# Seven products of halves for the last three experts' first layer, and the first batch's keys and values summed on TensorE

## The chip, the cores and the metric

The program runs on one core of one Trainium2 chip. The metric is the device time of one execution in microseconds. TensorE (PE) multiplies matrices and writes its results to PSUM, which has eight banks here (the tiles `pa`). VectorE (DVE), ScalarE (ACT) and GpSimd (POOL) do the elementwise work; GpSimd's work is all on SBUF. SyncE (SP) issues most DMA transfers, GpSimd the gathers and scatters.

## What is computed

Three stages follow each other on 4608 tokens of width 512.

```python
k_p, v_p = k.reshape(B, H, Sp, 8, D).mean(axis=3), v.reshape(B, H, Sp, 8, D).mean(axis=3)   # B, H, S, D = 8, 8, 576, 64
attn = softmax(q @ k_p.T / sqrt(D)) @ v_p
h = x @ w_in                                     # 512 to 2048
g = (a0 + a1*h + a2*h**2 + a3*h**3) / (1 + |b0|*|h| + |b1|*h**2 + 1e-6)
x = g @ w_out                                    # 2048 to 512
# each token goes to one of 8 experts, by the sorted gate scores, 576 tokens to an expert
for e in range(8):
    out[mask] = relu(x[mask] @ w1[e]) @ w2[e]    # 512 to 1024 to 512
```

## The kernel before

The kernel writes every operation, with its engine, an estimated duration and what it reads and writes, into a list. A planner (`Order.run`) then plays the list through with those estimates and fixes the order on each engine: among the operations that are ready it takes the one with the lowest priority number, which is the place in the list unless `prio` says otherwise. An operation written with `either` (as in `tt` and `cp`) goes to whichever of two engines the planner finds better. PSUM banks are given out by the planner too (`Dyn`). Any change in the list can therefore move the order of the work everywhere. Where the plan shows TensorE idle early on, matmuls on a tile of zeros (line 348) are put in.

A product in full precision is made of three matmuls in the faster 32-bit format (fp32r): each operand is split into a rounded part h and a remainder l, and h*h, h*l and l*h are added up in PSUM. A rounding is a ScalarE copy, a remainder a subtraction on VectorE or GpSimd.

**The start.** The attention of a batch is done in two units of four heads. For a unit the kernel loads keys (`load_k`, 0.59 MB), values (`load_v`, 0.79 MB in two transfers for the first batch) and queries (`load_q`, 0.26 MB for 256 tokens). `prep_k` sums the keys over groups of 8 with one reduction on VectorE (line 535) and scales them into `kbd`; `prep_v` sums the first batch's values by halves in three steps on GpSimd (line 553) and one reduction on VectorE (line 555), then rounds them. Scores (line 589), the maximum (line 593), exponentials on ScalarE (line 602) and transposes (line 624) follow. Keys of all units share the buffer `kvraw`, so unit 1's keys are requested when unit 0's are summed. The queue begins with a piece of the weights (0.52 MB), keys, queries and values of unit 0; the constants `cst` (0.09 MB, with the identity matrix and the polynomial's coefficients) come later, by `LATER = 60`. Small operations on the coefficients (lines 387 to 394) need them. Beside the attention, the weights of the next stage are rebuilt piece by piece from 64-bit numbers (`prep_w`).

**The middle.** The polynomial stage runs as 2 x 72 steps, with `act1` and `act2` on each. `mt` is a ring of three tiles (`MTB`) and `mr` one of two, later three (`MRB`, `MORE_R`), for the low part of its quotient; `ex` is a ring of two (`EXB`) for the exponentials.

**The experts.** `ffn(k)` does expert k: a first layer, with hidden features on the partitions in eight blocks f of 128 and the 576 tokens in two halves of 256 and 320 columns, then a second layer over five tiles of tokens (four of 128, one of 64). For one f and half there are twelve matmuls:

```python
products = (wh, yh), (wh, yl), (wl, yh)
...
    nc.tensor.matmul(ps()[:, 0:n], w()[:, c, fs], x()[:, c, :], start=i == 0, stop=i == 11)
```

`load` fetches a quarter of a weight matrix (0.52 MB), rounds it on ScalarE (line 1833) and takes the remainder on GpSimd (line 1837). The first layer's output is rounded with the ReLU (line 1922), its remainder taken on VectorE (line 1927). `begin(k + 1)` loads the next expert's first-layer weights while expert k is worked on, `fetch(k + 1)` gathers its tokens and `turn` transposes them on TensorE and splits them (8 column groups a pair of tiles of 128 on VectorE). Both weight matrices have rings of five quarters, the split tokens two sets. `route(k + 1)`, the choice of the next expert's tokens, is a long chain on VectorE that runs ahead of the experts and ends before the last three. `out` is written by a scatter from `ob` (line 1975).

Of the kernel before, what the change touches and what calls it, by code (L numbers as in the profile page):

```python
# [18 lines left out]
ALU = mybir.AluOpType  # L19
# [21 lines left out]
LATER = 60  # L41
W_FIRST = 1
MTB = 3
# [9 lines left out]
EXB, ENB = (2, 4)  # L53
# [251 lines left out]
class Kern:  # L305
# [172 lines left out]
    def init_att(self):  # L478
# [4 lines left out]
        self.dma(lambda: self.cst()[:, 0:170], lambda: self.a["cst"], 87040, w=[self.vmask, self.ident, self.wgate, (self.scal, 0), (self.scal, 1)], prio=LATER)  # L483
# [49 lines left out]
    def prep_k(self, b, u):  # L533
        nc, op, k, ks = self.nc, self.op, self.kvraw, self.ks
        op("DVE", c_tt(1152), lambda: nc.vector.tensor_reduce(
            ks(), k()[:, 0:2 * S].rearrange("p (c s j) -> p c s j", c=2, j=8), op=ALU.add, axis=AX.X), r=[k] + [(k, r) for r in range(4)], w=[ks])
        h = self.kbd[u]
        for r in range(2):
            o = lambda r=r: h()[64 * r:64 * r + 64, :, NK * r:NK * r + NK]
            i = lambda r=r: ks()[64 * r:64 * r + 64]  # L540
# [3 lines left out]
    def prep_v(self, b, u):  # L544
        nc, op, v, vs, vf = self.nc, self.op, self.kvraw, self.vs, self.vf
        vk = [v] + [(v, r) for r in range(4)]
        if b == 0:
            v, x = self.vhead[u]
            n, f4 = 8, lambda: v().rearrange("p (c x) -> p c x", c=2)
            while n > 1:  # L550
                n //= 2
                o = (lambda n=n: f4()[:, :, 0:n * D]) if n > 1 else (lambda: vs()[:, 0:2])
                op("Pool", p_tt(2 * n * D), lambda o=o, n=n: nc.gpsimd.tensor_tensor(
                    o(), f4()[:, :, 0:n * D], f4()[:, :, n * D:2 * n * D], op=ALU.add), r=[v], w=[v] if n > 1 else [vs])
# [14 lines left out]
        for r in range(2):  # L569
            def z(t, r=r):  # L570
                return t()[64 * r:64 * r + 64, 0:2, 64 * r:64 * r + 64]
            sv = lambda r=r: vs()[64 * r:64 * r + 64, 0:2, :]
            op("Act", c_act(128, 1), lambda z=z, sv=sv: nc.scalar.activation(z(h), sv(), AF.Copy), r=[vs], w=[(h, r)])
# [85 lines left out]
    def att_slots(self):  # L659
# [7 lines left out]
        def first():  # L667
            self.load_k(0, 0)
            self.load_q(0)
            self.load_v(0, 0)  # L670
            self.prep_k(0, 0)
            self.load_k(0, 1)
            for i in range(1, QB):
                self.load_q(i)
            self.load_v(0, 1)
# [1163 lines left out]

    def begin(self, k):  # L1840
# [6 lines left out]
        self.w1 = []  # L1847
        for j in range(4):
# [6 lines left out]
    def fetch(self, k):  # L1855

        nc, fop, ix = self.nc, self.fop, self.ix[k % 3]
        for c in range(5):
# [31 lines left out]
    def ffn(self, k):  # L1890
# [3 lines left out]
        for j in range(4):  # L1894
            d = (self.w2h[self.n2 % 5], self.w2l[self.n2 % 5])
            self.n2 += 1
            w2.append(d)
# [185 lines left out]
```

## Time and profile before

| | us |
|---|---|
| median of 3 runs | 1479.06 (1478.07 to 1480.18) |
| the profiled execution | 1474.23 |
| its span in the profile | 1472.5 |
| TensorE busy | 1436.0 (98%) |
| VectorE busy | 1056.0 (72%) |
| ScalarE busy | 910.8 (62%) |
| GpSimd busy | 859.3 (58%) |

Times in the profile count from the start of the span. A busy TensorE is not TensorE at its peak: a matmul's row is longer than the distance to the next one, since they overlap, and what a matmul costs is read from the distance of the starts. VectorE's rows overlap a little too. The granted clock is 1.00 when TensorE runs at full speed. An idle engine that nothing waits for costs nothing.

### The profile page before, as it was taken

Reading aid. Unit: us, or ns where it says so; the run is one execution under the profiler, and the core shown is the slowest. Engines: PE = TensorE matmul, PEld = TensorE weight load, DVE = VectorE, ACT = ScalarE, POOL = GpSimd, SP = SyncE. Lnnn points to the kernel's source line nnn. Section 1 sums busy time; section 2 is a strip of 40 time slices with the busy share of each in tenths; the row PEclk is TensorE's granted clock in tenths of the full one; section 3 lists DMA queues with packets and bytes.
Section 4 is the critical chain, followed back from the end, with each engine's and each line's share of the span. In section 5 each row is a group of like instructions: output and inputs, shape, how many; then the busy total and the mean of one; then the engine's idle time right before and its main releaser. Section 6 shows DMA issues by size and latency. Waiting matters only on the chain. (4 is left out here: it accounts for less than half of the span.)

```text
span 1472.5 us, 27165 instructions
## 1 busy us (share of the span) xinstructions
PE 1436.0 (98%) x9476; PEld 1298.5 (88%) x9476; DVE 1056.0 (72%) x2894; ACT 910.8 (62%) x2206; POOL 859.3 (58%) x806
## 2 busy tenths in 40 slices
PE   8899989999999999999999999999999999999998
PEld 7899879888898999988999899777888988988997
DVE  6987787868778698887767777987877877731220
ACT  6998877878868787766545565843454553543331
POOL 6878777667757465664445654743374653753521
PEclk9999999999999999999999999999999999999999
DMA  7663533242421444433233332014154433533300
GB/s 252 217 226 110 177 125 123 88 145 92 151 91 51 144 132 146 137 87 97 77 116 99 103 86 88 1 59 162 61 163 147 155 130 98 165 116 114 129 26 32
DMA packets 105941, 173.61 MB, mean 118 GB/s; under 512 B 8384, under 2 KB 72256, under 8 KB 105792
## 3 DMA queue, kind: packets, MB, share of 16 engines
q1 hardware_dynamic: 80896, 134.02, 27.5%
q0 software_dynamic: 24896, 37.76, 9.1%
q8 instruction: 75, 1.23, 0.3%
q14 instruction: 74, 0.61, 0.1%
HBM read 122.29 MB, written 49.46 MB: 117 GB/s over the span
## 5 line engine op out<-in xcount | busy, mean ns | idle before, releaser
L735 PE MATMUL pa<-xh,wih 128*128 128x256 f32 (+1 forms) x576 | 202.9, 352 | 7.8 <-DVE mt L792 5.8
L735 PE MATMUL pa<-xh,wil 128*128 128x256 f32 (+1 forms) x576 | 195.3, 339 | 0.7 <-POOL wil L362 0.7
L735 PE MATMUL pa<-xl,wih 128*128 128x256 f32 (+1 forms) x576 | 194.7, 338 | 0.0
L860 PE MATMUL pa<-woh,mg 128*128 128x260 f32 x480 | 130.3, 287 | 1.1 <-DVE mg L782 1.0
L362 POOL TENSOR_TENSOR mg<-mt,mr 128x512 fp32r<-128x512 f32 x75 | 96.9, 1293 | 56.6 <-DVE mt L792 39.0
L861 PE MATMUL pa<-wol,mg 128*128 128x260 f32 x480 | 128.3, 283 | 0.0
L735 PEld LDWEIGHTS pa<-xh,wih 128*128 128x128 f32 x576 | 109.4, 190 | 20.3 <-DVE mt L792 5.1
L1975 POOL DMA_INDIRECT out<-ob,ix x40 | 38.9, 973 | 151.0 <-ACT ob L1971 127.2
L735 PEld LDWEIGHTS pa<-xh,wil 128*128 128x128 f32 x576 | 109.2, 190 | 13.6 <-POOL wil L362 0.9
L735 PEld LDWEIGHTS pa<-xl,wih 128*128 128x128 f32 x576 | 109.5, 190 | 8.6
L792 DVE SCALAR_TENSOR_TENSOR mt<-pa,cst,mt 128x512 f32<-128x512 f32 x144 | 107.0, 744 | 10.5 <-POOL mt L788 9.8
L753 ACT ACTIVATE ms<-pa,cst 128x512 f32<-128x512 f32 x72 | 49.3, 684 | 98.1 <-PE pa L735 98.1
L602 ACT ACTIVATE ex<-pa,nm 128x72 f32<-128x72 f32 (+2 forms) x320 | 99.1, 331 | 9.7 <-DVE nm L593 9.3
L858 PE MATMUL pa<-woh,mg 128*128 128x260 f32 x480 | 105.0, 285 | 0.0
L765 DVE TENSOR_TENSOR mwq<-mwq,pa 128x512 f32<-128x512 f32 x96 | 65.3, 683 | 44.7 <-ACT pa L759 22.8
L1922 ACT ACTIVATE h2h<-pa 128x256 fp32r<-128x256 f32 (+1 forms) x128 | 51.2, 407 | 71.0 <-PE pa L1919 66.5
L1927 DVE SCALAR_TENSOR_TENSOR h2l<-pa,h2h 128x256 fp32r<-128x256 f32 x128 | 53.3, 418 | 55.8 <-ACT h2h L1922 49.0
L860 PEld LDWEIGHTS pa<-woh,mg 128*128 128x128 f32 x480 | 90.4, 188 | 2.4 <-DVE mg L782 1.9
L362 POOL TENSOR_TENSOR en<-ex,sm 128x256 f32<-128x256 f32 (+5 forms) x160 | 77.9, 508 | 24.8 <-DVE sm L608 12.3
L861 PEld LDWEIGHTS pa<-wol,mg 128*128 128x128 f32 x480 | 90.5, 188 | 0.3
L781 ACT ACTIVATE mr<-mr,cst 128x512 f32<-128x512 f32 x121 | 88.3, 730 | 1.5
L362 POOL TENSOR_TENSOR mwq<-mwq,ms 128x512 f32<-128x512 f32 x48 | 64.5, 1344 | 30.4 <-ACT mwq L763 30.1
(557 smaller groups left out, 5199.8 us busy)
## 6 DMA issues: line engine op xcount, KB each, us to landing
mwq<-in_w SPq DMA_DIRECT2D x42, 512.0 KB, 3.7
wraw<-in_w SPq DMA_DIRECT2D x22, 512.0 KB, 3.6
kvraw<-in_v SPq DMA_DIRECT2D x14, 768.0 KB, 4.9
ya_d<-ya SPq DMA_DIRECT2D x18, 520.0 KB, 3.6
yab<-ya_d SPq DMA_DIRECT2D x18, 520.0 KB, 4.3
kvraw<-in_kT SPq DMA_DIRECT2D x16, 576.0 KB, 4.4
x_d<-xh SPq DMA_DIRECT2D x18, 512.0 KB, 3.1
x_d<-xl SPq DMA_DIRECT2D x18, 512.0 KB, 4.5
```

The source lines that it names most:

```text
L362: self.g.either({"Pool": (p_tt(n), lambda: nc.gpsimd.tensor_tensor(out(), x(), y(), op=alu)), "DVE": (c_tt(n), lambda: nc.vector.tensor_te ...
L602: op("Act", c_act(NK, 0, 1, 1), lambda h=h: nc.scalar.activation(e()[:n, h, :], sv()[:, h, :], AF.Exp, bias=nm()[:n, h:h + 1], accum_out=s ...
L735: nc.tensor.matmul(o, w()[:, c, f], x()[:, c].rearrange("p b t -> p (b t)") if two else x()[:, c, :], start=c == 0 and k == 0, stop=c == 3 ...
L753: op("Act", c_act(N, 0, 1), lambda: nc.scalar.activation(s(), ph(), AF.Square, scale=self.b1r()), r=hk + self.sk, w=[s])
L765: op("DVE", c_tt(N), lambda: nc.vector.tensor_tensor(w(), w(), ph(), op=ALU.mult), r=hk, w=[w])
L781: op("Act", c_act(N, 1, 1), lambda: nc.scalar.activation(r(), r(), AF.Exp, scale=-1.0, bias=self.nls()), w=[r])
L792: op("DVE", c_stt(N), lambda: nc.vector.scalar_tensor_tensor(t(), w(), self.a0(), t(), op0=ALU.add, op1=ALU.subtract), r=[(w, 0), self.hri ...
L858: nc.tensor.matmul(o, lo()[:, f], w(woh), start=False, stop=last)
L860: nc.tensor.matmul(o, hi()[:, f], w(woh), start=first, stop=False)
L861: nc.tensor.matmul(o, hi()[:, f], w(wol), start=False, stop=False)
L1922: fop("Act", c_act(n), lambda hh=hh, t=t, n=n, ps=ps: nc.scalar.activation(hh()[:, t], ps()[:, 0:n], AF.Relu), r=[ps], w=[(hh, half)])
L1927: fop("DVE", c_stt(t1 - t0), lambda hh=hh, o=o, o0=o0, ps=ps, t0=t0, t1=t1, half=half: nc.vector.scalar_tensor_tensor(o()[:, o0:o0 + t1 - ...
```

## The change

It has two halves.

In the first layer of experts 5, 6 and 7 (`SEVEN = 5`) the product of the weights with the tokens is taken in halves: the weight matrix is cut in two along its input features (d) and in two along its hidden features (h), the tokens in two sets of 288 and their features in two. The four quarters of the output then follow from seven products of quarters in place of eight, of sums and differences of quarters (Winograd's form). `load_seven` loads a piece j, that is 128 features of each half, in two transfers, and makes three plain quarters and four combined ones, by four additions on VectorE; a slot holds the split results, and three slots serve four pieces. `turn_seven` transposes pairs of token tiles and makes seven token operands (22 column groups a pair on VectorE). `layer_seven` takes the seven products, each of 2 x 3 matmuls of 288 columns, and adds them up on VectorE with seven additions that read PSUM; the ReLU is taken in pieces of 256 and 32 columns. The buffers come from the old rings: the second-layer weights have four quarters in place of five from then on, the tokens one set.

In the first batch, unit 0's keys and both units' values (the part of 64 groups) are summed by eight matmuls with the identity matrix in fp32, into PSUM; the values' remainders are taken by VectorE alone. Unit 1's keys go to two other buffers (`ya`, `yap`), are loaded in the third place, and are reduced by two VectorE instructions. The constants are loaded first of all (`CST = -1`). The ring `mt` has two tiles, `ex` three. The last tile's copy at the very end is one ScalarE instruction and is no longer split between ScalarE and VectorE.

```diff
-MTB = 3
+CST = -1
+MTB = 2
-EXB, ENB = (2, 4)
+EXB, ENB = (3, 4)
...
     def load_k(self, b, u):
+        if (b, u) == (0, 1):
+            self.k01 = [View(t, lambda t: t.rearrange("p a n -> p (a n)")[:, 0:S]) for t in (self.ya, self.yap)]
+            for c, t in enumerate(self.k01):
+                self.dma(t, lambda c=c: self.a["kT"][b, u][:, c], 294912, w=[t])
+            return
...
     def prep_k(self, b, u):
+        if (b, u) == (0, 1):
+            for c, t in enumerate(self.k01):
+                op("DVE", c_tt(576), lambda c=c, t=t: nc.vector.tensor_reduce(
+                    ks()[:, c], t().rearrange("p (s j) -> p s j", j=8), op=ALU.add, axis=AX.X), r=[t], w=[(ks, c)])
...
+        elif b == 0:
+            def mm(i):
+                for j in range(2 * i, 2 * i + 2):
+                    nc.tensor.matmul(sv(), self.ident(), kv()[:, :, :, j], start=j == 0, stop=j == 7)
...
     def prep_v(self, b, u):
-                op("Pool", p_tt(2 * n * D), lambda o=o, n=n: nc.gpsimd.tensor_tensor(
-                    o(), f4()[:, :, 0:n * D], f4()[:, :, n * D:2 * n * D], op=ALU.add), r=[v], w=[v] if n > 1 else [vs])
+                for j in range(2 * i, 2 * i + 2):
+                    nc.tensor.matmul(ps()[:, 0:2 * D].rearrange("p (c d) -> p c d", c=2), self.ident(), f4()[:, :, D * j:D * j + D], start=j == 0, stop=j == 7)
+            for i in range(4):
+                op("PE", .5, lambda i=i: mm(i), r=[v, self.ident], w=[ps], prio=len(self.g.ops) + 60)
...
         def first():
             self.load_k(0, 0)
             self.load_q(0)
+            self.load_k(0, 1)
+            self.load_q(1)
             self.load_v(0, 0)
+            self.load_v(0, 1)
             self.prep_k(0, 0)
...
+    def load_seven(self, k, j):
+        for h in range(2):
+            op("SP", .06, lambda h=h: nc.sync.dma_start(rv()[:, :, h], src()[:, :, h, 128 * j:128 * j + 128]), r=[("reg", k)], w=[(raw, h)], nbytes=262144)
+        for i, (p, v, n) in enumerate(((p0, lambda: rv()[:, :, 0], 512), (p1, lambda: rv()[:, 2:4, 1], 256))):
+            op("Act", c_act(n, 1), lambda p=p, v=v: nc.scalar.activation(p(ah), v(), AF.Copy), r=both, w=[(ah, i)])
+            self.tt(n, lambda p=p: p(al), v, lambda p=p: p(ah), ALU.subtract, r=[*both, (ah, i)], w=[(al, i)])
+        q = lambda d, h: rv()[:, 2 * d:2 * d + 2, h]
+        for o, x, y, alu in (((1, 1), (0, 1), (1, 1), ALU.add), ((0, 1), (0, 0), (0, 1), ALU.subtract),
+                             ((0, 0), (1, 1), (0, 0), ALU.subtract), ((1, 0), (1, 0), (0, 0), ALU.subtract)):
+            op("DVE", c_tt(256), lambda o=o, x=x, y=y, alu=alu: nc.vector.tensor_tensor(q(*o), q(*x), q(*y), op=alu), w=both)
+        op("Act", c_act(1024, 1), lambda: nc.scalar.activation(sh(), raw(), AF.Copy), r=both, w=[(sh, 0)])
+        op("Pool", p_tt(1024), lambda: nc.gpsimd.tensor_tensor(sl(), raw(), sh(), op=ALU.subtract), r=[*both, (sh, 0)], w=[(sl, 0)])
...
+    def layer_seven(self, k, j, w, h2):
+        def product(ps, a, b):
+            for part in range(2):
+                def mm(part=part):
+                    for c in range(2):
+                        t, i = self.PLACES[b][c]
+                        for x, y in (((0, 0), (0, 1)), ((1, 0),))[part]:
+                            nc.tensor.matmul(ps()[:, 0:n], w[a][x][1](c), self.tokens[y][t]()[:, 288 * i:288 * i + 288], start=first, stop=last)
...
+        add = lambda out, ps, x: op("DVE", c_tt(n), lambda: nc.vector.tensor_tensor(v(out)(), v(ps)(), v(x)(), op=ALU.add), r=[y for y in (ps, x) if y is not out], w=[out])
+        product(P1, "A11", "B11")
+        op("Act", c_act(n), lambda: nc.scalar.activation(v(p1)(), v(P1)(), AF.Copy), r=[P1], w=[p1])
+        product(P6, "S2", "T2")
+        add(u2, P6, p1)
+        product(P2, "A12", "B21")
+        add(P2, P2, p1)
+        product(P7, "S3", "T3")
+        add(u3, P7, u2)
+        product(P5, "S1", "T1")
+        add(u2, P5, u2)
+        add(P5, P5, u3)
+        product(P4, "A22", "T4")
+        add(P4, P4, u3)
+        product(P3, "S4", "B22")
+        add(P3, P3, u2)
+        for ps, f, half in ((P2, j, 0), (P5, j + 4, 1), (P4, j + 4, 0), (P3, j, 1)):
...
     def begin(self, k):
+        if k >= SEVEN:
+            if k == SEVEN:
+                self.init_seven()
+            self.w1 = [self.load_seven(k, j) for j in range(3)]
+            return
...
     def ffn(self, k):
+        for j in range(4 if k >= SEVEN else 0):
+            self.layer_seven(k, j, w1[j], h2)
+            if j == 0:
+                w1.append(self.load_seven(k, 3))
...
+                if k + 1 >= SEVEN and 0 < c < 4:
+                    self.turn_seven(k + 1, c - 1)
...
-            if k + 1 == E and at == 4:
-                fop("Act", c_act(256), lambda ob=ob, ps=ps: nc.scalar.activation(ob()[:, 0:256], ps()[:, 0:256], AF.Copy), r=[ps], w=[ob])
-                fop("DVE", c_tt(256), lambda ob=ob, ps=ps: nc.vector.tensor_copy(ob()[:, 256:512], ps()[:, 256:512]), r=[ps], w=[(ob, 1)])
-            elif n == 128:
+            if n == 128:
```

## Rows read from the trace of the kernel before

**Rows 1.** Stretch of expert 5's first layer: us, PE, PEld, DVE, ACT, POOL, clock, DMA, GB/s

```profile
1308.80:1334.20 25.40, 25.40 (x193) 25.40 (x192) 7.95 (x24) 11.97 (x22) 21.52 (x11) 1.00 0.55 177
```

**Rows 2.** Timeline of TensorE, experts 4 and 5: start, us, engine, line, operation, times

```profile
1256.75 1.60 PE L1919 MATMUL pa<-xh,xl 128*128 128x256 f32 x12
1258.18 0.31 PE L1919 MATMUL pa<-ythb,xl 128*128 128x320 f32 x1
...
1259.95 0.40 PE L1919 MATMUL pa<-xh,woh 128*128 128x256 f32 x2
...
1308.77 0.64 PE L1919 MATMUL pa<-yth,wih 128*128 128x256 f32 x4
...
1334.21 0.39 PE L1953 MATMUL pa<-xl,h2h 128*128 128x512 f32 x1
1334.44 0.40 PE L1953 MATMUL pa<-xl,h2l 128*128 128x512 f32 x1
```

**Rows 3.** Stretches of the start, columns as in rows 1

```profile
5.00:10.00 5.00, 3.85 (x34) 3.30 (x32) 3.77 (x6) 1.45 (x5) 1.34 (x2) 1.00 1.01 361
10.00:15.00 5.00, 3.71 (x34) 3.08 (x32) 2.83 (x11) 3.85 (x21) 4.84 (x7) 1.00 1.04 396
15.00:20.00 5.00, 4.53 (x35) 3.78 (x36) 4.94 (x11) 3.75 (x11) 4.69 (x9) 1.00 0.62 200
20.00:25.00 5.00, 4.55 (x36) 3.66 (x35) 4.88 (x13) 3.36 (x17) 3.60 (x6) 1.00 0.79 245
30.00:35.00 5.00, 4.55 (x41) 4.39 (x41) 2.90 (x11) 3.05 (x14) 4.83 (x6) 1.00 0.37 109
...
85.00:110.00 25.00, 25.00 (x213) 25.00 (x213) 21.42 (x41) 22.02 (x49) 16.66 (x17) 1.00 0.64 219
```

**Rows 4.** Groups by form, TensorE, 0 to 100 us: busy us, mean ns, idle before

```profile
L348 PE MATMUL pa<-idle 128*128 128x256 bf16 x158 | 21.9, 290 | 3.9 <-ACT ex L602 2.4 <-POOL idle L318 1.0 <-DVE wf L437 0.5
```

**Rows 5.** Timeline of all engines, 0 to 60 us; in brackets idle before and releaser

```profile
6.47 1.35 DVE L535 TENSOR_REDUCE ks<-kvraw 128x144 f32<-128x1152 f32 x1
...
8.66 1.26 POOL L553 TENSOR_TENSOR mwq<-mwq 128x512 f32<-128x512 f32 x1 [6.15 <-DMA mwq<-in_v]
...
15.48 1.35 DVE L535 TENSOR_REDUCE ks<-kvraw 128x144 f32<-128x1152 f32 x1
...
16.74 0.15 DVE L391 RECIPROCAL cst<-cst 128x1 f32<-128x1 f32 x1
...
18.42 2.13 PE L589 MATMUL pa<-kbd,qraw 128*128 128x144 f32 x16
```

**Rows 6.** Groups by form, VectorE, whole span

```profile
L1641 DVE TENSOR_TENSOR pa<-cc,pa 128x288 f32<-128x288 bf16 x6 | 2.7, 453 | 0.0
```

**Rows 7.** Timeline of VectorE in expert 5's first layer

```profile
1312.63 0.42 DVE L1927 SCALAR_TENSOR_TENSOR h2l<-pa,h2h 128x256 fp32r<-128x256 f32 x1 [1.39 <-ACT h2h L1922]
1312.97 0.21 DVE L1927 SCALAR_TENSOR_TENSOR h2h<-pa,h2h 128x64 fp32r<-128x64 f32 x1
```

**Rows 8.** Instructions on the tile mt, 90 to 950 us: ns min/median/max, first and last start

```profile
L792 DVE SCALAR_TENSOR_TENSOR mt<-pa,cst,mt x134: 729/743/752, 89.5 to 946.6; 128x512 f32<-128x512 f32 x134
...
L790 DVE SCALAR_TENSOR_TENSOR mt<-mwq,cst,mg x32: 734/752/1925, 98.0 to 587.1; 128x512 f32<-128x512 f32 x32
...
L790 DVE SCALAR_TENSOR_TENSOR mt<-mq,cst,mg x16: 746/1192/2319, 107.4 to 593.6; 128x512 f32<-128x512 f32 x16
```

**Rows 9.** Timeline of GpSimd in expert 5

```profile
1308.44 2.40 POOL L1837 TENSOR_TENSOR wol<-wraw,woh 128x1024 fp32r<-128x1024 f32 x1
```

**Rows 10.** Timeline of the end

```profile
1458.10 0.60 ACT L1971 ACTIVATE ob<-pa 128x512 f32<-128x512 f32 x1 [4.98 <-PE pa L1950]
...
1458.97 0.97 POOL L1975 DMA_INDIRECT out<-ob,ix  x1 [3.42 <-ACT ob L1971]
...
1467.26 0.42 DVE L1969 COPY ob<-pa 128x256 f32<-128x256 f32 x1 [4.17 <-PE pa L1950]
...
1468.43 0.97 POOL L1975 DMA_INDIRECT out<-ob,ix  x1 [4.16 <-ACT ob L1968]
```

More of the change, by code (lines that the diff above doesn't have):

```diff
@@ L1838, in load, with init_seven, tokens @@
                 r=[raw, h] + ([self.ix[0], ("y", LATE[-1], 1)] if k == 0 else []), w=[l])
+    def init_seven(self):
+        flat = lambda t: View(t, lambda t: t.rearrange("p a b -> p (a b)"))
+        n1, n2, at = self.n1, self.n2, lambda q, n: [x[n % 5] for x in q]
+        w1, w2 = (self.w1h, self.w1l), (self.w2h, self.w2l)
+        old = [*at(w1, n1), *at(w2, n2), *(x for j in range(4) for x in at(w1, n1 - 4 + j))]
+        self.w2x = [tuple(at(w2, n2 - 4 + j)) for j in range(4)]
+        new = [flat(t) for t in old]
+        self.slots = [new[4 * s:4 * s + 4] for s in range(3)]
+        for s in range(3):
+            self.op("Z", 0.0, lambda: None, w=[*old[4 * s:4 * s + 4], ("slot", s)])
+            for t in self.slots[s]:
+                for k in range(2):
+                    self.g.lastw[t, k] = self.g.lastw["slot", s]
+        self.npiece = 0
+        def tokens(q):
+            old = [q[1][0], q[1][1], q[0][0], q[0][1]]
+            new = [flat(t) for t in old]
+            self.op("Z", 0.0, lambda: None, w=[(t, c) for t in old for c in range(5)] + [("tok", q is self.ytl)])
+            for t in new:
+                for i in range(4):
+                    for c in range(3):
+                        self.g.lastw[t, i, c] = self.g.lastw["tok", q is self.ytl]
+            return new
+        self.tokens = [tokens(q) for q in (self.yth, self.ytl)]
@@ L1857, in fetch @@
         nc, fop, ix = self.nc, self.fop, self.ix[k % 3]
-        for c in range(5):
+        for c in (0, 2, 1, 3, 4) if k >= SEVEN else range(5):
             n = 128 if c < 4 else 64
@@ L1899, in ffn @@
             h2.append((self.h2h[f], self.h2l[f]))
-        for turn in [[(f, half)] for half in range(2) for f in range(8)] if k == 0 else [[(f, 0), (f, 1)] for f in range(8)]:
+        for j in range(4 if k >= SEVEN else 0):
+            self.layer_seven(k, j, w1[j], h2)
+            if j == 0:
+                w1.append(self.load_seven(k, 3))
+        for turn in [] if k >= SEVEN else [[(f, half)] for half in range(2) for f in range(8)] if k == 0 else [[(f, 0), (f, 1)] for f in range(8)]:
             for f, half in turn:
@@ L1936, in ffn @@
             if k + 1 < E:
-                for j in TURNS[c]:
+                if k + 1 >= SEVEN and 0 < c < 4:
+                    self.turn_seven(k + 1, c - 1)
+                for j in TURNS[c] if k + 1 < SEVEN else ():
                     self.turn(k + 1, j)
@@ L2009 @@
 PER = 1
+SEVEN = 5
 @with_exitstack
```

112 lines of the change are left out of this document (99 added, 13 removed).

## The prediction

> **What bounds the kernel now.** I read three views: busy time in stretches, the timeline of the first 35 us, and the timeline of the last experts. In the last three experts nothing but TensorE counts. Over the first layer of expert 5 it is busy 25.40 of 25.40 us at a granted clock of 1.00, which is the 2.4 GHz level, while VectorE has 7.95 us of work and GpSimd 21.52 [rows 1]. Its matmuls follow each other without a gap: twelve of 256 columns take 1258.18 - 1256.75 = 1.43 us (0.119 each), the next twelve of 320 take 1259.95 - 1258.18 = 1.77 us (0.1475 each) [rows 2]. The price is thus by the column (465 ns and 461 ns per thousand), and any column taken out there comes off the end.
>
> The start is another matter. Between 10 and 35 us the engines wait for each other. In 15 to 25 us VectorE is full (4.94 and 4.88 of 5) while ScalarE idles 1.25 and 1.64 us; in 10 to 15 ScalarE idles 1.15 and VectorE 2.17; in 30 to 35 both idle, 1.95 and 2.10 [rows 3]. TensorE's busy time there is mostly padding: 21.9 us of it are 158 matmuls on a tile of zeros [rows 4]. So early on the end is set by how soon VectorE and ScalarE get their work. What they wait for is data: unit 1's keys use the buffer of unit 0's, so they are requested only when those have been summed (at 6.47 us, for 1.35), and are summed at 15.48 [rows 5].
>
> **The seven products.** In experts 5 to 7 the first layer had 8 x 12 x (256 + 320) = 55,296 columns; seven products of 2 x 3 matmuls of 288 columns, four times, are 48,384, which is 7/8. The transposes stay at twenty. A first layer lasts 1334.21 - 1308.77 = 25.44 us [rows 2], and there are three: 76.3 / 8 = **-9.5 us** if TensorE is fed. A layer would then last 22.3 us, a piece of it (one j) 5.6.
>
> What feeds it is VectorE, with seven additions of 288 columns per piece that read PSUM. The nearest row takes 453 ns [rows 6]; the next instruction starts about 0.08 us before a row's end (1312.97 - 1312.63 = 0.34 for a 0.42 row [rows 7]), so 0.37 each, 2.6 us per piece. Four remainders of 256 columns at 0.34 add 1.4, four of 32 columns (0.13 from the row of 64 columns, 0.21 less 0.08) add 0.5. That is 4.5 us per piece, 17.9 per layer, against 22.3 of TensorE. Beside it run the four additions that combine the fourth piece's weights, 4 x 0.37 = 1.5. ScalarE and GpSimd get more roundings and remainders per piece; ScalarE's work before is half a layer (11.97 of 25.40 [rows 1]), and it is costed at nothing. If its cover went, the ReLU copies would hold the banks that the next piece's products want.
>
> These weight additions read both inputs from SBUF, a kind that the last experts do not have now. Earlier in the trace such an instruction (line 790) takes 746 ns at best, 1192 in the median of one form and 2319 at worst, but 752 in the median of the commoner form, while line 792, of like size with one input from PSUM, stays within 729 to 752 [rows 8]. The long ones look like waits for GpSimd. An add in a layer where GpSimd is busy 21.52 of 25.40 us [rows 1], with remainders of 2.40 us [rows 9], may thus wait for nothing or for a whole 2.40. I take 0.5 us, near the 0.45 by which the slower form's median exceeds its best: 4 x 0.5 = 2.0 per layer. VectorE then has 17.9 + 1.5 + 2.0 = 21.4 of 22.3. It fits with 0.9 to spare, which is little for a queue whose every step waits for TensorE or ScalarE.
>
> By the Trainium skill, page "SBUF — State Buffer", section "Who interferes with whom", a VectorE instruction with two SBUF inputs contends with a GpSimd instruction that reads SBUF, and whichever starts first blocks the other fully; the trace's 746 to 2319 agrees. Taken at its harshest, with every add behind a remainder, the whole sum would be +7.5 (the rival called the lock, below) in place of the -10.5 by the row's usual price.
>
> Two places are late next. The fourth piece's weights go into the slot that the first piece leaves, 5.6 us into the layer, and are wanted at 16.7; in between lie four adds (1.5 + 2.0), remainders of 2.40 and, by their columns, 1.2 and 0.6 on GpSimd, and two ScalarE steps, some 9 of 11 us. And the last product's outputs are needed by the second layer's fourth pair of matmuls, which follow each other at 0.23 (1334.44 - 1334.21 [rows 2]), so some 1.4 us after the layer ends; the order may fill that gap with the next tile. I allow 0.7 us per expert for both: **+2.1**. Bounds: 0 (all fits), and 4 x 2.40 + 17.9 + 1.5 - 22.3 = 6.7 per expert if every add waits out a remainder.
>
> The tokens' preparation grows from 8 to 22 column groups per tile pair on VectorE. It lies in the second layer, with two tiles still to go when its last third starts (24 + 16 matmuls at 0.23, some 9 us), for expert 5 beside the last of the routing; nothing, and what would be late is the next expert's first product. Each weight piece takes two transfers in place of one, 12 more on SP's queue; they are wanted a piece later, so nothing. The second-layer weights lose their spare buffer: their first rounding waits until the previous expert's last tile is done, a whole first layer ahead of use; nothing.
>
> **The end.** The last copy out was split: VectorE started at 1467.26, ScalarE followed, and the scatter was issued at 1468.43, 1.17 us later. A whole copy by ScalarE took 1458.97 - 1458.10 = 0.87 from its start to the scatter [rows 10]: **-0.3**.
>
> **The start.** The keys of unit 1 now stand behind 2.05 MB of transfers (constants 0.09, weights 0.52, keys 0.59, queries 0.26, themselves 0.59) in place of 4.39. At 361 to 396 GB/s [rows 3], 0.38 MB per us, they land 6.2 us earlier: about 9.3 in place of 15.5. Unit 0's values move the other way, from 1.90 to 2.84 MB: 2.5 us later than 8.66 [rows 5]. The second weight piece moves 0.68 MB back, 1.8 us, its preparation with it.
>
> The first keys' sum on TensorE is eight fp32 matmuls of 144 columns, 16 records; such a group of 16 takes 2.13 us against 1.35 for VectorE's reduction [rows 5]. With the constants' 0.09 MB ahead (0.2 us) the first scores come 1.0 us later. ScalarE, which follows them, idles longer than that before 35 us.
>
> Out of VectorE's full stretch go 1.35 us (unit 1's keys, into the idle 10 to 15) and ten small setup steps of 0.15 like the one at 16.74 [rows 5], since the constants now land first: 1.5. In come four remainders of the values, 0.2 to 0.3 each by the rows of 64 and 288 columns: 1.0. Net -1.85. GpSimd loses six sums, the longest 1.26 [rows 5], and the value sums take TensorE time that is padding now. With unit 1's exponentials earlier I add half of ScalarE's idle at 30 to 35, 0.95. Sum **-2.8**. Bounds: +1.0, if the later first scores simply pass through, and -5.0, ScalarE's idle in 10 to 25 and 30 to 35 (6.0) less that 1.0. From 85 us on TensorE is full again (25.00 of 25 [rows 3]), so the gain should reach the end.
>
> Of the ring sizes, three score tiles in place of two cost nothing. Two mt tiles in place of three cost nothing in the first half, where the two mr tiles already hold a step until the remainder two steps back is done; in the second half GpSimd would have to fall more than a whole step behind.
>
> **Sum.** -9.5 + 2.1 - 0.3 - 2.8 = -10.5. The profiled execution took 1474.23 us (span 1472.5), so it would take 1463.7; on the median of 1479.06, 4.8 above it, that is **1468.6**.
>
> **Rivals.** *All idle recovered:* VectorE keeps up and the start gives its bound: -9.5 - 0.3 - 5.0 = -14.8, 1464.3. For it: VectorE's 17.9 of 22.3, and the 6.2 us by which the keys come early. Against: the values come 2.5 us later. *The start gives nothing:* its later first scores pass through: -9.5 + 2.1 - 0.3 + 1.0 = -6.7, 1472.4. For it: the second weight piece and the values are delayed; against: ScalarE's idle. *The chain in the layer:* every step waits for another engine, and half of the 9.5 is lost: -9.5 + 4.8 - 0.3 - 2.8 = -7.8, 1471.3; with the rival before it, 1475.1. *The lock (other side):* every weight add in a layer waits a whole remainder, +6.7 x 3 = 20.1: +7.5, 1486.6. It decides from 12.6 / 3 = 4.2 us over per layer, which is 1.8 us per add; the row's median speaks against that.
>
> **Numbers.** Forecast 0.48 (own range 1466 to 1471.5), all idle recovered 0.22, the start gives nothing 0.15, the chain 0.08, the lock 0.07. Range 1463.5 to 1475.5. Within 0.2% (3 us) is about what a measurement of this kernel can tell from no change. The first four cases end faster unless two of them meet (0.03); the lock is slower in most of its cases: faster 0.90, same 0.05, slower 0.05.
>
> **What would show it.** First layers of experts 5 to 7 of 22.3 to 23.2 us on TensorE without idle; VectorE near 21 us in each. Weight adds mostly at 0.4 us, a few above 2. Unit 1's keys reduced near 9.5 us, first scores near 9.7, VectorE's small setup steps before 6. From 100 to 1280 us the same work, shifted by some 3 us; a second layer of unchanged length. The prediction is wrong if TensorE idles in those layers, if the shift at 100 us is absent or lost by 500, or if the stretch from 100 to 1280 changes its own length, since the order of all work is planned anew.

## The result, and the profile after

The changed kernel took 1489.01 us (1486.33 to 1491.99, six runs) beside 1478.57 for the kernel before on the same chip: a ratio of 1.0069, 95% interval 1.0054 to 1.0084. It is slower by 10 us where 10.5 us less was forecast. The profiled execution took 1487.33 us (span 1485.4).

**The last experts.** The stretches of the changed kernel's last three experts come first: first and second layer of expert 5, of expert 6, first layer of expert 7 (columns as in [rows 1]).

```profile
1314.60:1341.50 26.90, 24.96 (x175) 24.50 (x174) 21.47 (x61) 13.60 (x40) 19.54 (x15) 0.94 0.38 124
1341.50:1370.80 29.30, 28.49 (x133) 22.45 (x133) 20.45 (x48) 14.86 (x38) 20.83 (x16) 1.00 0.38 114
1370.80:1398.95 28.15, 24.58 (x169) 23.54 (x169) 18.34 (x55) 13.03 (x40) 19.35 (x15) 0.94 0.36 116
1398.95:1428.70 29.75, 28.53 (x134) 22.48 (x133) 22.33 (x50) 14.77 (x38) 18.96 (x14) 1.00 0.34 102
1428.70:1454.05 25.35, 22.99 (x169) 22.43 (x168) 17.66 (x55) 11.58 (x36) 14.44 (x9) 1.00 0.17 58
```

Before, such a first layer took 25.40 us with TensorE busy throughout [rows 1]. Now they take 26.90, 28.15 and 25.35, TensorE is idle for 1.94, 3.57 and 2.36 of them, and in two of them the granted clock is 0.94 where it was 1.00. VectorE, the third number after the comma, has 21.47, 18.34 and 17.66 us of work, about the 21.4 that were forecast or less. From the start of expert 5's first layer to the last matmul the changed kernel needs 165.4 us, the kernel before 158.5: +7.0, where -7.4 was forecast for these layers. TensorE's waits between 1259 and 1482 us say on whom it waits (waited for, us in total, times, longest):

```profile
PE pa L1987 <- DVE ob L1992: 4.1, 2, 3.0
PE pa L1987 <- DVE gt L1992: 2.8, 2, 1.5
PE pa L2142 <- DVE h2h L2015: 2.0, 2, 1.2
```

So VectorE, with time to spare in every layer, comes late. Its timeline with GpSimd's and TensorE's shows two kinds of stop. First expert 6 (start, us, engine, line, operation; in brackets idle before and releaser):

```profile
1376.36 2.41 POOL L1869 TENSOR_TENSOR w2l<-mwq,w2h 128x1024 fp32r<-128x1024 f32 x1
1378.94 0.93 POOL L2161 DMA_INDIRECT out<-ob,ix  x1 [0.17 <-issue]
...
1382.54 0.46 DVE L1992 TENSOR_TENSOR ob<-pa,gt 128x288 f32<-128x288 f32 x1 [4.03 <-DMA out<-ob,ix]
...
1383.05 0.40 PE L1987 MATMUL pa<-ythb,wih 128*128 128x288 f32 x1 [3.03 <-DVE ob L1992]
```

The sum U3 is kept in the other output buffer (`self.ob[(5 * k + 1) % 2]`). The previous expert's last scatter still reads that buffer. Its issue stood on GpSimd behind a remainder of 2.41 us, and VectorE could write 3.6 us after it. VectorE held still for 4.03 us, TensorE for 3.03. Expert 7 has the same wait of 3.39. In expert 5 the instruction in front is the list of a later expert (line 1768), 3.03 us late here. The kernel before has that wait too (3.41 us, at 1317.83, where the trace names such a scatter as its end), but TensorE was not idle there [rows 1]. The second kind of stop stands right behind it:

```profile
1322.31 0.16 DVE L1768 SCALAR_TENSOR_TENSOR ix<-ts,pa 128x5 int32<-128x5 f32 x1 [3.03 <-issue]
1322.39 0.45 DVE L1992 TENSOR_TENSOR ob<-pa,gt 128x288 f32<-128x288 f32 x1
1322.75 2.23 DVE L1920 TENSOR_TENSOR mwq<-mwq 128x256 f32<-128x256 f32 x1
1324.90 0.44 DVE L1992 TENSOR_TENSOR gt<-pa,gt 128x288 f32<-128x288 f32 x1
...
1322.27 2.41 POOL L1869 TENSOR_TENSOR w2lr<-mwq,w2hr 128x1024 fp32r<-128x1024 f32 x1
...
1327.19 1.06 PE L1987 MATMUL pa<-xh,xl 128*128 128x288 f32 x6 [1.54 <-DVE gt L1992]
```

The weight addition (line 1920) ends 0.3 us after the GpSimd remainder that began 0.5 us before it. Over all 48 of them (the instructions of a line: ns min, median, max):

```profile
L1920 DVE TENSOR_TENSOR mwq<-mwq x32: 383/418/2412, 1268.0 to 1444.4; 128x256 f32<-128x256 f32 x32
...
L1920 DVE TENSOR_TENSOR wraw<-wraw x16: 406/424/2281, 1290.8 to 1417.0; 128x256 f32<-128x256 f32 x16
...
L1992 DVE TENSOR_TENSOR pa<-pa,ob x36: 444/449/466, 1317.8 to 1454.3; 128x288 f32<-128x288 f32 x36
```

16 of the 48 took over 0.6 us, and each of these ended 0.27 to 0.30 us after the end of an elementwise instruction of GpSimd that ran beside it. The other 32 took at most 0.47; one that had only the issue of a transfer on GpSimd beside it took 0.42 (at 1268.77). The additions that read PSUM (line 1992, the largest of its groups is shown) never exceeded 0.47. The stops are then paid a second time, in clock. TensorE in expert 5 after its two idle spells, and the granted clock there in stretches of 2 us (sixth number after the comma):

```profile
1328.89 0.30 PE L1987 MATMUL pa<-ytlb,xh 128*128 128x288 f32 x1
1329.02 0.29 PE L1987 MATMUL pa<-ythb,xh 128*128 128x288 f32 x1
...
1329.94 0.44 PE L1987 MATMUL pa<-ytlb,wih 128*128 128x288 f32 x1
1330.18 0.44 PE L1987 MATMUL pa<-ythb,wih 128*128 128x288 f32 x1
```

```profile
1328.00:1330.00 2.00, 1.60 (x10) 1.37 (x10) 2.00 (x8) 0.67 (x4) 1.64 (x2) 0.84 0.84 275
1330.00:1332.00 2.00, 2.00 (x10) 2.00 (x10) 2.00 (x6) 1.92 (x4) 0.88 (x1) 0.50 0.14 55
1332.00:1334.00 2.00, 2.00 (x15) 2.00 (x14) 1.84 (x8) 1.18 (x7) 2.00 (x2) 0.81 0.00 0
```

Matmuls of 288 columns start 0.13 us apart at 2.4 GHz, and 0.24 apart for some 3 us at 1.2 GHz. Expert 6 has such a spell after its 3.03 us of idle, expert 7, with idle spells of 1.05 and 1.31, has none.

**The start.** TensorE and VectorE of the changed kernel:

```profile
7.31 4.32 PE L557 MATMUL pa<-kvraw,cst 128*128 128x144 f32 x16
12.67 1.64 PE L622 MATMUL pa<-kbd,qraw 128*128 128x144 f32 x12
14.14 1.95 PE L580 MATMUL pa<-mwq,cst 128*128 128x128 f32 x16
...
16.42 1.95 PE L580 MATMUL pa<-mwq,cst 128*128 128x128 f32 x16
```

```profile
8.31 0.75 DVE L544 TENSOR_REDUCE ks<-ya 128x72 f32<-128x576 f32 x1 [0.34 <-DMA ya<-in_kT]
...
9.05 0.75 DVE L544 TENSOR_REDUCE ks<-yap 128x72 f32<-128x576 f32 x1
13.37 0.95 DVE L626 TENSOR_REDUCE nm<-pa 128x4 f32<-128x288 f32 x2 [3.57 <-PE pa L622]
```

Unit 1's keys are there as early as forecast. But the sum of unit 0's keys takes 4.32 us, at a granted clock of 1.00, not the 2.13 of [rows 5], and the first scores come at 12.67 in place of 8.67. VectorE idles 3.57 us for them. The polynomial stage's first matmul moves from 35.50 to 36.72, its 145th (the one that the expectations below call the 144th) from 98.05 to 103.53, and the experts' first from 1024.38 to 1028.77. After TensorE has been idle for 0.22 and 2.42 us (until 25.43), its granted clock is 0.52 from 26 to 29 us; the kernel before has 1.00 there.

**The end.** The last copy starts at 1480.10 and the scatter is issued 0.88 us later (1.17 before [rows 10]), as forecast. But the span ends 4.4 us after that issue, and 4.1 in the kernel before, so that the 0.3 us does not show in this execution's length.

### The profile page after: what moved, and what is told of

It reads as the page before. It is cut to its first block, busy times and chain, and to the rows that moved or that the text cites. A ratio compares the mean times of both kernels' runs of the same rounds, so it can differ in the third digit from the quotient of the medians.

```text
span 1485.4 us, 27526 instructions
## 1 busy us (share of the span) xinstructions
PE 1440.8 (97%) x9431; PEld 1298.4 (87%) x9431; DVE 1136.2 (76%) x3121; ACT 935.8 (63%) x2338; POOL 889.3 (60%) x827
## 5 line engine op out<-in xcount | busy, mean ns | idle before, releaser
L892 PEld LDWEIGHTS pa<-woh,mg 128*128 128x128 f32 x480 | 90.4, 188 | 2.0 <-DVE mg L814 1.5
L1453 DVE TENSOR_SCALAR_CACHE_REDUCE BJ<-BQ,cand 128x288 uint16<-128x288 f32 x154 | 76.9, 510 | 6.3 <-ACT BQ L1638 4.4
L890 PEld LDWEIGHTS pa<-woh,mg 128*128 128x128 f32 x480 | 77.1, 188 | 4.1 <-POOL mg L363 3.0
```

Source lines behind the costliest of these rows:

```text
L890: nc.tensor.matmul(o, lo()[:, f], w(woh), start=False, stop=last)
L892: nc.tensor.matmul(o, hi()[:, f], w(woh), start=first, stop=False)
L1453: D(.43, lambda: self.nc.vector.tensor_scalar(j(), key(), cand(), None, op0=ALU.is_lt if less else ALU.is_ge, op1=ALU.add, accum_out=self. ...
```

## The experiments

The theory had three causes: U3's buffer, the weight additions beside GpSimd, and the keys' sum on TensorE. Ratios are to the kernel before in runs on the same chip (its medians 1477.4 to 1479.4). Five groups of kernels ran on a chip each time: seven_only, seven_u3, seven_both and head_only; seven_pool, seven_one, head_contig and head_dve; rings, head_contig_rings, head_noval and combo_contig; seven_both_again, head_k01, combo_k01 and combo_noval; combo_p1 and combo_p1_ix.

| kernel | us | ratio, 95% interval |
|---|---|---|
| seven_only | 1485.95 | 1.0048, 1.0030 to 1.0066 |
| seven_u3 | 1482.11 | 1.0020, 1.0002 to 1.0037 |
| seven_pool | 1479.84 | 1.0017, 1.0005 to 1.0028 |
| seven_both | 1474.83 | 0.9974, 0.9959 to 0.9988 |
| seven_both_again | 1475.53 | 0.9989, 0.9977 to 1.0001 |
| seven_one | 1478.40 | 1.0007, 0.9995 to 1.0018 |
| head_only | 1483.08 | 1.0030, 1.0017 to 1.0043 |
| head_contig | 1477.32 | 1.0000, 0.9989 to 1.0011 |
| head_dve | 1480.46 | 1.0014, 1.0002 to 1.0026 |
| head_noval | 1474.39 | 0.9979, 0.9966 to 0.9991 |
| head_k01 | 1476.10 | 0.9985, 0.9974 to 0.9995 |
| rings | 1476.55 | 0.9996, 0.9982 to 1.0009 |
| head_contig_rings | 1480.78 | 1.0024, 1.0011 to 1.0037 |
| combo_contig | 1476.64 | 0.9992, 0.9979 to 1.0006 |
| combo_k01 | 1473.29 | 0.9962, 0.9947 to 0.9977 |
| combo_noval | 1470.77 | 0.9950, 0.9936 to 0.9964 |
| combo_p1 | 1473.49 | 0.9973, 0.9960 to 0.9986 |
| combo_p1_ix | 1476.20 | 0.9989, 0.9975 to 1.0003 |

seven_both and seven_both_again are the same kernel, so ratios from two groups can differ by 1.5 thousandths with no change at all, and the intervals do not cover that. One of seven_u3's ten runs took 3589 us; without it its median is 1481.48. Single profiled executions scatter too: six versions whose start is that of the kernel before reached the polynomial stage's 145th matmul between 97.1 and 98.7 us, but the experts' first matmul between 1024.8 and 1030.9. For differences of a few us the ratios decide, and the traces only say what stopped whom.

**The two halves apart.** seven_only is the kernel before with the seven products (and the single last copy); head_only has `SEVEN = 8`, which no expert reaches.

> The seven products alone, on the start of the kernel before. If the loss of the changed kernel adds up from its places as its trace shows them (first layers of experts 5 to 7 and the second layers between them 7.0 us longer in all than before), this run is about 7 us slower than the kernel before, with first layers of about 27, 28 and 25 us. If the loss is one of the newly planned order elsewhere, it is within 3 us of before.

> The new start, rings and end alone, with the first layers of all experts as before. If the start costs what the changed kernel's trace shows between 98 and 762 us (5.5 and 4.6 us late), this run is 4 to 6 us slower than before. If the start was as forecast and only disturbed by the rest, it is 3 us faster.

Both as the theory had it: +4.8 and +3.0 thousandths, 7.1 and 4.4 us, together 11.5 where the whole change costs 10.2 (0.69% of 1478.57).

**The two stops in the layers.**

```diff
-p1, u2, u3 = self.ob[5 * k % 2], self.gt[4], self.ob[(5 * k + 1) % 2]
+p1, u2, u3 = self.ob[5 * k % 2], self.gt[4], self.u3          # seven_u3, seven_both
...
-op("DVE", c_tt(256), ... nc.vector.tensor_tensor(q(*o), q(*x), q(*y), op=alu), w=both)
+op("Pool", p_tt(256), ... nc.gpsimd.tensor_tensor(q(*o), q(*x), q(*y), op=alu), w=both)   # seven_pool, seven_both
```

> The seven products alone, with a buffer of its own for the second partial sum (u3), so that VectorE no longer waits for the scatter that reads ob. If that wait (3.0 us in expert 5, 4.4 in expert 6) is half of the loss, each first layer gets 2 to 3 us shorter and the run is 6 to 9 us faster than seven products alone. If VectorE simply has more work than fits, the layers keep their length within 1 us.

> As the run before it, and the weights are combined on GpSimd, so VectorE never has two inputs in SBUF there. If stops of VectorE's queue are the whole cause, the first layers come to 22.3 to 23.5 us without idle of TensorE and the run is 6 to 9 us faster than the kernel before. If VectorE has too much work, or GpSimd gets too much (some 10 us more per expert), layers stay above 25 us.

> The seven products alone, with the four weight additions of each piece on GpSimd, and the sum U3 still in the output buffer that the previous expert's last scatter reads. Theory: the two stops are separate. The scatter's stop stays (VectorE's addition into ob waits 2 to 4 us for DMA out<-ob, twice), the long additions of 2.4 us are gone. Of the 11.1 us between the version with neither mended (1485.95) and that with both (1474.83), the buffer alone gave 3.8, so this one should stand near 1478 to 1480, about level with the kernel before. Rival (the additions are all, the buffer only mattered because the additions queue behind it): 1475 +- 1. Rival (GpSimd, now with 0.74 us more per addition, issues the scatter later still): above 1481.

> The seven products with both stops mended and the start as before, a second time and beside the combined versions. Theory: 3.5 to 5 us under the kernel before again (1472.5 to 1474). Rival (the first time was a lucky chip or execution): 0 to 2 us under it, 1475.5 to 1477.5.

Either cure alone leaves it slower than before, by 2.0 and 1.7 thousandths; both together make it faster, by 2.6 the first time and 1.1 the second, where the interval just reaches no change. Alone, each cure is worth some 3 thousandths (4 us), and on top of the other 2.8 to 4.6, so they are two stops. The traces agree: TensorE's wait for the sum in `ob`, 4.5 us in two waits in seven_only, is gone in seven_u3, where it waits 5.1 us in three for VectorE's remainders; with both cures no wait of TensorE in the last three experts is over 1.3. seven_pool was level with its expectation, the others fell short of theirs by 1 to 5 us, and the 1475.53 of seven_both_again lies at the edge of its rival (a lucky first time), not in the range of its theory. What is left in seven_both shows in its stretches (first layer of expert 5, second, first of expert 6, second, first of expert 7):

```profile
1310.10:1333.95 23.85, 22.54 (x170) 22.30 (x169) 15.82 (x52) 13.10 (x40) 23.30 (x21) 1.00 0.38 117
1333.95:1362.70 28.75, 28.47 (x135) 22.52 (x134) 10.86 (x39) 14.05 (x37) 25.68 (x25) 1.00 0.36 115
1362.70:1388.65 25.95, 23.87 (x170) 22.52 (x169) 16.53 (x53) 13.45 (x40) 24.73 (x21) 1.00 0.44 138
1388.65:1416.90 28.25, 28.25 (x134) 22.49 (x133) 10.16 (x37) 14.69 (x39) 26.26 (x25) 1.00 0.27 89
1416.90:1439.70 22.80, 22.54 (x169) 22.30 (x168) 15.97 (x51) 12.04 (x36) 15.46 (x12) 1.00 0.30 87
```

GpSimd, with additions of 0.74 us each, is now nearly full in expert 6 (24.73 of 25.95); where it is not, in expert 7, the layer takes 22.80. The clock stays at 1.00 throughout. Expert 6 has the longest first layer in every version but seven_pool, 24.8 to 30.5 us.

**What makes the additions wait.**

```diff
-nc.vector.tensor_tensor(q(*o), q(*x), q(*y), op=alu)
+nc.vector.tensor_scalar(q(*o), q(*x), 1.0, None, op0=ALU.mult)
```

> The seven products with U3's own buffer, and the four weight additions of each piece left on VectorE but reading one operand only (a multiplication by 1.0 in place of the addition of two tiles), so that the sums of the weights, and the output, are left out. VectorE keeps 48 instructions of 128x256, at the same places of its queue and with the same waits. Theory (an addition of two tiles in SBUF waits for a GpSimd instruction in progress): each of the 48 now takes 0.2 to 0.5 us and none 2.4, and the time is that of the version with the additions on GpSimd or a little less, 1473 to 1475. Rival (the additions were long or late because VectorE's queue, the raw pieces or ScalarE's copies hold them there): it stays at 1481 to 1483.

The theory failed in its narrow form. With one input the instruction still waits (instructions of line 1890, then the longest of them with GpSimd and TensorE beside it):

```profile
L1890 DVE TENSOR_SCALAR mwq<-mwq x32: 250/284/3323, 1268.4 to 1437.1; 128x256 f32<-128x256 f32 x32
...
L1890 DVE TENSOR_SCALAR wraw<-wraw x16: 273/283/4337, 1288.3 to 1408.9; 128x256 f32<-128x256 f32 x16
```

```profile
1377.37 4.34 DVE L1890 TENSOR_SCALAR wraw<-wraw 128x256 f32<-128x256 f32 x1 [2.27 <-POOL wol L363]
...
1377.29 2.37 POOL L1839 TENSOR_TENSOR w2lr<-mwq,w2hr 128x1024 fp32r<-128x1024 f32 x1
1379.62 1.93 POOL L363 TENSOR_TENSOR xh<-mwq,xh 128x512 fp32r<-128x512 f32 x2
...
1382.19 1.33 PE L1957 MATMUL pa<-xh,wih 128*128 128x288 f32 x4 [3.04 <-DVE h2h L1985]
```

It began 0.08 us after a GpSimd instruction and ended at 1381.7, 0.16 us after the last of the three that followed each other there: it waited for all of them in a row. So it is not the second input: both kinds of instruction from SBUF to SBUF that were tried here, with two inputs and with one, wait for elementwise instructions of GpSimd. Other kinds were not tried. The Trainium skill, page "SBUF — State Buffer", section "Who interferes with whom", counts tensor_scalar among those that can contend, in a mode that uses both ports; this run agrees. The time, between that of seven_u3 and that of seven_both, fits neither number that was expected.

**The keys' sum.** In head_contig the eight summands of a key lie 72 columns apart, so the matmul reads runs of 72 in place of every eighth element; in head_dve VectorE sums the keys as before.

```diff
-kv = lambda: k()[:, 0:2 * S].rearrange("p (c s j) -> p c s j", c=2, j=8)
+kv = lambda: k()[:, 0:2 * S].rearrange("p (c j s) -> p c s j", c=2, j=8)     # head_contig
...
-        elif b == 0:
+        elif False:                                                          # head_dve
```

> The start of the changed kernel without the seven products, and unit 0's keys of the first batch laid out by the host with the eight summands of a key apart by 72 columns, so that TensorE's moving operand is read as runs of 72 in place of every eighth element; all else the same. Theory (TensorE was slowed by the stride of 32 bytes): the 16 records of the keys' sum take 2.1 to 2.3 us in place of 4.3, the first scores begin 2.0 to 2.3 us earlier (at 10.4 to 10.7), and 1.5 to 2.5 us of the 3.7 come back: 1480.5 to 1482 where the kernel before has 1479.4. Rival (fp32 columns from that tile are slow whatever the stride, or the clock is low there): the records stay above 4 us and the time at 1483. Rival (the start's length does not pass on to the end): records fast, time 1483.

> The start of the changed kernel without the seven products, and unit 0's keys of the first batch summed by VectorE in one instruction of 1152 elements as before; the values' sums stay on TensorE, unit 1's keys and the loads where the change has them. Theory (what the start loses is the keys' sum on TensorE): the first scores begin at 8.5 to 9.5 as before, the polynomial stage's 144th matmul is no later than before (98.05) or up to 2 us earlier, and the time is 1477 to 1479.5, level with the kernel before or up to 2.5 us under it. Rival (it loses by the order of the rest: the values' sums, the filters' remainders or the unit 1 keys ahead of them): the first scores are early and the 144th matmul still 3 us or more late, time 1482 to 1483.

The stride is the cause of the 4.32 us: the order on TensorE is the same in head_only and head_contig, and the clock in the sum is 1.00 in both. In head_contig's timeline of TensorE the same 16 records take 2.20 us:

```profile
7.15 2.20 PE L557 MATMUL pa<-kvraw,cst 128*128 128x144 f32 x16
10.38 1.64 PE L622 MATMUL pa<-kbd,qraw 128*128 128x144 f32 x12
```

3.0 thousandths, the whole loss of the start, come back, more than expected. The spell of low clock may be the rest: head_only has 0.74 and 0.69 from 23 to 29 us, head_contig 1.00; that was not tested apart. By the Trainium skill, page "Advanced Engine Details and Errata", section "SBUF Cachelines", accesses that fall on another 16-byte line each time pay a penalty; with elements 32 bytes apart each does, and 4.32 against 2.20 agrees. head_dve refutes the theory that this sum is all: its first scores come at 9.87, its first polynomial matmul at 32.42 (35.50 before), and yet it is 1.4 thousandths slower, with the 145th at 103.60, as its rival had it.

**The values' sums, and neither sum.** head_noval is head_contig with `prep_v` of the kernel before; head_k01 has neither sum on TensorE, only the second unit's keys elsewhere, the loads' order, the early constants and the rings.

> The start of the changed kernel without the seven products, the keys read in runs of 72, and the values of the first batch folded on GpSimd as before; the rest of the start as in the change. Theory (the 32 records of the values, 3.9 us of TensorE, are work added between the first scores and the polynomial stage): the first scores stay at 10.4, the first polynomial matmul comes no later than 32.77, and the time is 1475 to 1477.5. Rival (moving the values off GpSimd is the half of the start that pays): the first probabilities wait for the values, the first polynomial matmul is at 34 to 36 and the time 1479 to 1482.

> The start of the changed kernel without the seven products and without either sum on TensorE: unit 0's keys summed by VectorE, the values folded on GpSimd, both as before; unit 1's keys in the two other tiles, the order of the loads, the early constants and the rings as in the change. Theory (the two sums on TensorE are the start's loss, the second unit's keys and the loads its gain): 1473 to 1476, 2 to 4 us under the kernel before. Rival (the gain needs the keys' sum on TensorE, which spares VectorE 1.35 us at 6.5): level with the kernel before or above, 1477 to 1480.

With the values back on GpSimd both ways of summing the keys become faster by 2.1 to 2.9 thousandths, 3 to 4 us. That is the price of the values' sums on TensorE; how it arises is not shown. head_noval's theory had the first polynomial matmul no later than 32.77, and it comes at 38.66 (37.10 in head_k01); but the 145th comes at 90.33 (93.87), 7.7 us (4.2) before that of the kernel before. So the sums are not simply 3.9 us of TensorE put in ahead of the polynomial stage: with them the planner makes another order of the whole start. What then remains of the start, the early keys, loads and constants with the new rings and the single last copy, is worth 1.5 to 2.1 thousandths.

**The rings.** rings is the kernel before with `MTB = 2` and `EXB = 3`; head_contig_rings is head_contig with the old sizes.

> The kernel before with the two ring sizes of the change alone (two buffers mt in place of three, three buffers ex in place of two). Theory that the prediction used (the rings hold nothing up): 1478 to 1479.5, no difference by over 0.2%, and the 144th matmul of the polynomial stage within 1 us of 98.05. Rival (the rings, by the order that the planner makes with them, are what the start loses after its first polynomial matmul, where all three starts of the change took 66.8 us or more for 144 matmuls and the kernel before 62.55): the 144th matmul 3 us or more late, time 1481 to 1483.

> The start of the changed kernel without the seven products, the keys read in runs of 72, and the two rings as in the kernel before (three mt, two ex). Theory (the rings are innocent): as with the rings of the change, 1476.5 to 1479, the 144th matmul at 99 to 100. Rival (the rings cost the 4.2 us between the first and the 144th polynomial matmul): first one at 32 to 33 and the 144th at 95 to 96.5, time 1473 to 1475.5, which would be a start that beats the kernel before by the 2.8 us that the prediction named.

Alone they do nothing (its 145th matmul was even 4.3 us early, and nothing of that reached the end). With the new start the old sizes cost 2.4 thousandths more, against both expectations. The order on TensorE differs from about its 130th instruction on; which wait it is stays open.

**Versions with both halves mended.** combo_contig, combo_k01 and combo_noval are the whole change with both cures of seven_both and the start of the head version of that name.

> The whole change with the three causes mended: U3 in a buffer of its own, the weight additions on GpSimd, unit 0's keys of the first batch read in runs of 72. Theory (start and last experts add up): 4.6 us from the experts and 0 to 1 from the start, 1473 to 1474.8. Rival (the start passes its own loss of up to 1.5 us on): 1475 to 1477. The first layers of experts 5, 6 and 7 take 24, 26 and 23 us as in the version without the start.

> The change with U3 in its own buffer, the weight additions on GpSimd, and neither sum of the start on TensorE. Theory: the start's gain of the run with neither sum, plus 4 to 4.6 us of the experts: 1468.5 to 1472. Rival (interaction): 1473 to 1476.

> The change with U3 in its own buffer, the weight additions on GpSimd, unit 0's keys read in runs of 72 on TensorE, and the values folded on GpSimd as before. Theory (start and experts add up): 3 us from the start and 4 to 4.6 from the experts, 1469 to 1471.5. Rival (they share a bound between them, or the experts' 4.6 us was chance): 1473 to 1475.

combo_noval is the fastest of all, 7 us under the kernel before (in five runs), and fits its theory: -2.1 of the start and -1.1 to -2.6 of the experts against -5.0 thousandths. combo_contig (-0.8) and combo_k01 (-3.8) came out at the times of their rivals, though the same sums give -1.1 to -2.6 and -2.6 to -4.1 for them. That start and experts add up is thus likely, and not shown to better than a thousandth or two. The first layers of combo_noval:

```profile
1308.85:1332.25 23.40, 22.68 (x169) 22.34 (x168) 15.63 (x51) 13.10 (x40) 22.86 (x21) 1.00 0.37 116
...
1361.20:1388.80 27.60, 24.48 (x169) 23.90 (x168) 16.48 (x52) 14.20 (x41) 26.13 (x22) 0.94 0.46 138
...
1417.05:1439.25 22.20, 22.20 (x170) 22.19 (x168) 16.49 (x52) 12.65 (x38) 15.65 (x12) 1.00 0.25 82
```

In expert 7 TensorE is busy 22.20 of 22.20 us: the layer that the forecast had at 22.3. Expert 6 still waits 2.1 us, for ScalarE's copy of P1 into an output buffer. The last two runs went after it:

```diff
-p1, u2, u3 = self.ob[5 * k % 2], self.gt[4], self.u3
+p1, u2, u3 = self.p1, self.gt[4], self.u3
...
-self.ix = self.ring(3, "rt", [128, 5], I32, "ix")
+self.ix = self.ring(4, "rt", [128, 5], I32, "ix")              # combo_p1_ix alone
```

> The best combination so far (U3 in its own buffer, additions on GpSimd, keys on TensorE in runs of 72, values folded on GpSimd; 1470.77) with ScalarE's copy of P1 in a buffer of its own too, so that nothing of the seven products touches the output buffers. Theory: TensorE's wait for ScalarE's ob, 2.1 us, is gone, and 1 to 2 us with it: 1468.8 to 1470. Rival (what takes its place is the list ix or GpSimd): 1470.5 to 1471.5.

> The same with four lists ix in place of three, so that the list of expert 7 no longer waits for the scatter of expert 4's last tile in the middle of VectorE's queue. Theory: another 0.5 to 1 us: 1468 to 1469.5. Rival (it waits at a place where TensorE has products in hand): as without it.

Both missed. The wait for ob is gone from combo_p1's trace, but VectorE's remainders came in its place (2.2 us in two waits), in combo_p1_ix a late rounding of a weight piece by ScalarE (3.3). Neither is faster than combo_noval. combo_p1 has the same order on TensorE as combo_noval and one buffer more, and yet stands at -2.7 on another chip, so the -5.0 may flatter that kernel. What sets expert 6's layer is not settled.

## Why the prediction was wrong

**The step that failed first is "It fits with 0.9 to spare".** The sum before it was not too small: VectorE had 21.4 us forecast and 21.47, 18.34 and 17.66 measured. That expert 5 comes so near is chance, since seven weight additions fall into its layer in place of four (three are the next expert's), and four of the 16 remainders outside it. The allowance of 0.5 us for each weight addition was generous (0.80 in the mean over a median of 0.42, so 0.38). But the sum says nothing of single stops. What counts is the longest stop in VectorE's queue against the products that TensorE has in hand, and there stood additions of 2.2 to 2.4 us and waits of 3.0 to 4.0.

**The allowance of +2.1 missed the largest stop.** It had the fourth weight piece, for which no wait of TensorE shows, and the hand-over to the second layer, which alone cost 2.0 us (0.81 at 1344.70 and 1.22 at 1402.57, for the remainders). The largest stop was a scratch sum in an output buffer behind the previous expert's scatter. The prediction followed each new instruction's cost, but not each new buffer's last reader. That was shown by seven_u3.

**The clock was not in the sum.** Of the 80.4 us of the three first layers, 66.6 are three times the 22.20 of a layer that TensorE fills (combo_noval's expert 7), 7.9 are idle, and 5.9 are more busy time, of which the lower clock makes an estimated 3.3 (0.06 of 26.90 and of 28.15). With -9.5 and +2.1 the three layers should have lasted 68.9; they lasted 11.5 more. The second layers, forecast as unchanged, grew by 3.1 in all (1.4 and 1.7 in experts 5 and 6), 2.0 of it the hand-over.

**The -9.5 itself was right as a price by the column,** but seen only in one layer of three. With both stops mended 1.1 to 2.6 thousandths (1.6 to 3.8 us) arrive; from the start of expert 5's first layer to the last matmul the two traces show 2.9 and 3.3 us less than before.

**The start's -2.8 had two wrong prices and one right one.** The keys' sum was priced at 2.13 us by a row of as many columns, whose operand lay contiguous; it took 4.32. "The value sums take TensorE time that is padding now" was the other: nothing was charged for them, and they cost 3 to 4 us, by a way that stays open. The bound of +1.0 for the start was too narrow accordingly, the start as made costs +4.4. The second unit's keys, reduced at 8.31 and 9.05 where 9.5 was forecast, and the loads are worth 2.2 to 3.1 us as measured by head_k01 and head_noval; only those have the sign of the -2.8.

**The rings at nothing** hold for the kernel before, not for the new start. **The end's** -0.3 is there up to the scatter's issue and not beyond it.

**The rivals.** The lock had the right mechanism and the right side, and its 1486.6 lies near 1489.0, but not for its reason: the additions did not each wait a whole remainder (32 of 48 waited for little or nothing), about half of the experts' loss was the buffer, the clock came on top, and the start, which it still credited with -2.8, lost 4.4.

## What to carry to other kernels

When work moves onto an engine with time to spare, don't compare sums. List what can stop its queue (for each buffer it writes, who reads it last, and what that reader is queued behind; for each instruction from SBUF to SBUF, what GpSimd runs then) and compare the longest stop with the work that TensorE has in hand. Price a moved operation by a row with the same access pattern, not only with as many columns, and do not take padding on TensorE as free: here the work put into it cost 3 to 4 us.

## What was not expected of the hardware

A fp32 matmul with a moving operand read at every eighth element took 0.27 us a record in place of 0.14 (4.32 and 2.20 us for 16). A one-input multiplication from SBUF to SBUF waited 4.3 us for three GpSimd instructions in a row (2.37 us, then 1.93 for the other two), though 0.25 us was its best. After idle spells of 1.54 and 0.40 us in expert 5, and of 3.03 in expert 6, TensorE was granted half its clock for about 3 us; after 1.05 and 1.31 in expert 7, and 0.56 and 2.08 in head_contig's start, it was not.
